# First attention divided by its row sums ahead of the transposes, and the first pair's operands loaded over two queues

## The chip, the cores and the metric

The kernel runs on one core of one Trainium2 chip. The metric is device time in microseconds of one execution, the median of several runs. The engines are named as the profile names them: PE is TensorE (its matmuls) and PEld its weight loads, DVE is VectorE, ACT is ScalarE, POOL is GpSimd, SP is SyncE; SPq and ACTq are the instruction queues of SP and ACT, from which DMAs are issued.

## What is computed

Two attentions in a row. The first has 8 batches of 8 heads, 576 rows of 64 elements, and keeps only scores within `tau` of the row's maximum; the second is a mixture of four single-head causal attentions, with a gate that picks two of them for each row.

```python
def _attn_ref(q, k, v, tau):                      # q, k, v: 8 x 8 x 576 x 64
    scores = scale * np.matmul(q, k.transpose(0, 1, 3, 2))
    thresh = np.max(scores, axis=-1, keepdims=True) - tau
    scores = np.where(scores >= thresh, scores, -1e9)
    attn = np.exp(scores - np.max(scores, axis=-1, keepdims=True))
    attn = attn / (np.sum(attn, axis=-1, keepdims=True) + 1e-09)
    return np.matmul(attn, v)
...
def _moe_ref(x, w_gate, wq, wk, wv, wo):          # x: 8 x 576 x 512, 4 experts
    ...
    for e in range(E):                            # causal attention per expert
        q, k, v = x @ wq[e], x @ wk[e], x @ wv[e]
        ...
        ye = a @ v @ wo[e]
        # added to out with the gate's weight where e is among the row's two best
```

## The kernel before

Work on the first attention goes by pair: two heads of one batch, 32 pairs in all (index `n`). A pair's queries and keys are loaded (`load`, line 304), transposed on PE (`tr_in`, line 1108) and split into a high and a low part (`prep`, line 314: `in_hi` and `in_lo` out of PSUM, or `in_raw`, `flat_hi` and `flat_lo` for pairs 1 to 5), because a product of two floats is made of three PE products, high by high, high by low and low by high. `scores(n, s)` (line 331) handles one of five tiles of query rows, in the order `TS = (4, 2, 3, 0, 1)`: tiles 0 to 3 are 128 rows for each of the two heads (two rows of work, `j` = 0 and 1, each 128 partitions by 576 keys), tile 4 holds the last 64 rows of both heads in one such row. That makes nine rows of 128x576 per pair, 288 in all. Each row is taken out of PSUM by DVE with its minimum (`s_min`, line 1175; keys are scaled negatively, so a minimum is the maximum), goes through exp on ACT (`s_exp`, line 1189), and is masked and summed on DVE by `s_stt` (line 1192, instruction at line 1194). The masked row is then transposed on PE (`tr_pp`, line 1239 by way of `turn`) and copied out of PSUM (`out_t`), and `attnv` (line 363) multiplies it with the values.

The division by the row sums is folded in afterwards. For each of the two groups of tiles of a pair, `GROUPS = ((4, 2, 3), (0, 1))`, the sums lie in a small buffer `sg`; `g_sum` adds the epsilon and `g_inv` inverts (line 1202), `g_wide` and `g_tail` spread the inverses over 128 columns each into `iw` (by way of `copy`), `tr_inv` transposes `iw` on PE (line 1077), `iv_out` copies it from PSUM into `iv`, and `x_mul` (line 1277) and `x_tail` (line 1281) multiply the transposed output of `av` by it while taking that out of PSUM. `x_hi`, `x_lo` and `x_two` split the product for the second attention.

`second(b)` runs after each batch's four pairs: projections, values, gate, scores, exp, a division of its own by row sums ahead of its transposes (`add_eps`, `inv`, `share`, `scale2` at line 1487), transposes, products with the values, and the output projection. Where both halves of the array write one accumulation (`crossed`, line 273), PE runs the first half, a tiny instruction on DVE, ACT or POOL (`fence`, line 1348) waits for it, and the second half waits for that.

The order of all instructions is written out by hand. Every task belongs to a family (`pt`, `iw`, `s`, ...); the table `ORDER` gives each task of a family its place in one global order, and `BY` gives one digit per task that names its engine where there is a choice. What a digit stands for follows from the call: for `evac` 0 is ACT and 1 DVE; for `moved` 0 POOL, 1 ACT, 2 DVE; for `small` and the fences 0 DVE, 1 ACT, 2 POOL; for the row scaling 0 POOL, 1 DVE, 2 ACT. `plan` (line 157) only assigns buffers and emits in that order, with some filler matmuls on PE during the first 23 us by its own count. Buffers are few: 8 PSUM banks (kinds `s` and `d` take two, `g` one) and the slots of `SLOTS`.

The first pair's keys are loaded by five DMAs from SP's queue, its queries by five from ACT's (line 306); all later loads go through SP. All of these DMAs are issued at line 1090.

## Time and profile before

| | |
|---|---|
| median of 3 runs | 832.75 us (831.75 to 833.85) |
| the profiled execution | 832.69 us |
| its span, first to last instruction | 831.0 us |
| granted TensorE clock, mean | 0.997 of full speed |
| busy share of the span | PE 97%, PEld 92%, DVE 88%, ACT 79%, POOL 34% |
| DMA | 43.18 MB, mean 52 GB/s |

A share of busy time is an average over the whole span; the stages of this kernel differ, and the rows below give them by stage. PE's matmuls are pipelined and their ends are modelled, so PE's busy time overstates what one group of matmuls costs the next; the starts of the weight loads (PEld) show at what pace PE moves on. Instructions of one engine may overlap by the fill of its pipeline, so a duration is a little longer than the step from one to the next.

### The profile page before, as it was taken

Reading aid. Unit: us, or ns where it says so; the run is one execution under the profiler, and the core shown is the slowest. Engines: PE = TensorE matmul, PEld = TensorE weight load, DVE = VectorE, ACT = ScalarE, POOL = GpSimd, SP = SyncE. Lnnn points to the kernel's source line nnn. Section 1 sums busy time; section 2 is a strip of 40 time slices with the busy share of each in tenths; the row PEclk is TensorE's granted clock in tenths of the full one; section 3 lists DMA queues with packets and bytes.
Section 4 is the critical chain, followed back from the end, with each engine's and each line's share of the span. In section 5 each row is a group of like instructions: output and inputs, shape, how many; then the busy total and the mean of one; then the engine's idle time right before and its main releaser. Section 6 shows DMA issues by size and latency. Waiting matters only on the chain.

```text
span 831.0 us, 35075 instructions
## 1 busy us (share of the span) xinstructions
PE 808.6 (97%) x14472; PEld 763.1 (92%) x14472; DVE 733.6 (88%) x2327; ACT 653.5 (79%) x1374; POOL 280.9 (34%) x604
## 2 busy tenths in 40 slices
PE   9989999999999999999999999999999999989998
PEld 7888999999989998899999999989998899988997
DVE  6999999998899889899988999998999988889474
ACT  4999779976898679887689767898679877779465
POOL 5756504412332124521235231521133422231451
PEclk9999999999999999999999999999999999999999
DMA  4433212122121212122112321113022113110002
GB/s 108 97 85 79 51 35 47 32 61 50 30 69 44 79 44 46 33 52 46 30 44 63 90 70 30 39 32 97 22 60 60 27 55 76 33 40 3 15 27 78
DMA packets 135632, 43.18 MB, mean 52 GB/s; under 512 B 130608, under 2 KB 130608, under 8 KB 135472
## 3 DMA queue, kind: packets, MB, share of 16 engines
q1 hardware_dynamic: 134240, 40.64, 20.1%
q8 instruction: 114, 1.87, 1.0%
q10 hardware_dynamic: 1232, 0.30, 0.2%
q14 instruction: 46, 0.38, 0.2%
HBM read 31.47 MB, written 9.44 MB: 49 GB/s over the span
## 4 chain that ended last, share of the span: by engine, by line
PE 75%; DVE 14%; ACT 7%; issue 3%; SPq 1%; DMA 1%; POOL 0%; DVEq 0%; ACTq 0%; POOLq 0%
PE ps L1087 61%; PE ps L1239 7%; PE ps L1077 6%; DVE e L1194 4%; DVE e L1177 4%; ACT pt L1063 2%; ACT e L1190 1%; DVE e L1464 1%; ACT e L1469 1%; SPq L1090 1%; DVE kk L1134 1%; DVE iv L1277 1%; ACT pa L1063 1%; DMA qi<-in_q_dram 0%; DVE pt L1065 0%
## 5 line engine op out<-in xcount | busy, mean ns | idle before, releaser
L1190 ACT ACTIVATE e<-e,sm 128x576 f32<-128x576 f32 x288 | 214.4, 770 | 24.0 <-DVE e L1177 23.2
L1177 DVE TENSOR_SCALAR_CACHE_REDUCE e<-ps 128x576 f32<-128x576 f32 x288 | 209.5, 752 | 21.4 <-PE ps L1087 16.6
L1194 DVE SCALAR_TENSOR_TENSOR e<-e,sm,e 128x576 f32<-128x576 f32 x256 | 204.7, 818 | 4.3 <-ACT e L1190 2.6
L1087 PE MATMUL ps<-kk,qq 64*128 64x288 f32 x1920 | 175.4, 306 | 3.1 <-DVE e L1177 1.8
L1063 ACT ACTIVATE pt<-ps 128x640 f32<-128x640 f32 (+3 forms) x234 | 146.5, 644 | 27.1 <-PE ps L1239 19.0
L1087 PE MATMUL ps<-pt,vm 128*64 128x128 f32 (+1 forms) x1536 | 155.9, 258 | 0.0
L1087 PEld LDWEIGHTS ps<-kk,qq 64*128 64x128 f32 x1920 | 141.2, 186 | 9.0 <-DVE e L1177 3.5
L1087 PE MATMUL ps<-pa,vm 128*64 128x128 f32 x1024 | 135.8, 276 | 1.0 <-DVE kk L1134 0.5
L1087 PEld LDWEIGHTS ps<-pt,vm 128*64 128x64 f32 x1536 | 131.1, 137 | 0.0
L1239 PE MATMUL ps<-ident,e 64*128 64x64 f32 x2624 | 124.2, 226 | 4.9 <-DVE e L1177 2.3
L1239 PEld LDWEIGHTS ps<-ident,e 64*128 64x128 f32 x2624 | 107.8, 139 | 14.9 <-DVE e L1177 4.3
L1087 PEld LDWEIGHTS ps<-pa,vm 128*64 128x64 f32 x1024 | 111.9, 137 | 6.1 <-DVE kk L1134 0.7
L1087 PE MATMUL ps<-x,wh 64*128 64x288 f32 x1024 | 106.6, 296 | 0.3 <-ACT pa L1063 0.2
L1087 PEld LDWEIGHTS ps<-x,wh 64*128 64x128 f32 x1024 | 86.1, 185 | 1.1 <-DVE e L1177 0.4
L1063 ACT ACTIVATE pa<-ps 128x512 f32<-128x512 f32 x114 | 67.0, 594 | 21.7 <-PE ps L1239 18.8
L1087 PE MATMUL ps<-x,wl 64*128 64x288 f32 x512 | 80.2, 292 | 0.0
L1492 POOL TENSOR_SCALAR e<-e,sm 128x384 f32<-128x384 f32 (+4 forms) x104 | 62.0, 604 | 36.8 <-DVE sm L1235 23.6
L1469 ACT ACTIVATE e<-e,sm 128x128 f32<-128x128 f32 (+3 forms) x128 | 70.8, 556 | 3.2 <-DVE sm L1464 2.8
L1464 DVE CUSTOM_DVE_ANT_0 e<-ps,tri 128x128 f32<-128x128 f32 (+3 forms) x128 | 58.7, 484 | 5.2 <-PE ps L1087 4.6
L1087 PE MATMUL ps<-wh,x 64*128 64x260 f32 x576 | 60.8, 285 | 0.0
L1071 POOL TENSOR_TENSOR x<-iv,x 128x64 fp32r<-128x64 f32 (+2 forms) x67 | 44.8, 678 | 41.9 <-ACT x L1063 27.9
L1087 PE MATMUL ps<-pt,vt 128*64 128x128 f32 (+1 forms) x640 | 58.9, 262 | 0.0
(163 smaller groups left out, 1650.2 us busy)
## 6 DMA issues: line engine op xcount, KB each, us to landing
vm<-in_v_dram SPq DMA_DIRECT2D x64, 128.0 KB, 2.6
out_dram<-ob SPq DMA_DIRECT2D x32, 256.0 KB, 2.4
ki<-in_k_dram SPq DMA_DIRECT2D x96, 64.0 KB, 2.4
qi<-in_q_dram SPq DMA_DIRECT2D x62, 80.0 KB, 2.4
ki<-in_k_dram SPq DMA_DIRECT2D x32, 80.0 KB, 2.5
vt<-in_v_dram SPq DMA_DIRECT2D x128, 16.0 KB, 2.1
qi<-in_q_dram SPq DMA_DIRECT2D x31, 64.0 KB, 2.3
qi<-in_q_dram SPq DMA_DIRECT2D x31, 48.0 KB, 2.5
```

Source lines behind the costliest of these rows:

```text
L1063: self.nc.scalar.activation(dst, src, AF.Copy)
L1071: eng.tensor_tensor(dst, a, b.bitcast(F32), op=ALU.subtract)
L1077: self.nc.tensor.transpose(self.ps[:, bank, c * n:(c + 1) * n], x[sl], self.ident[sl, sl])
L1087: return self.nc.tensor.matmul(out, x, y, start=first, stop=last)
L1090: (self.nc.sync if e == "SP" else self.nc.scalar).dma_start(dst, src)
L1177: self.nc.vector.tensor_scalar(self.sides(sc), self.dbank(s)[:, :, :HS], 0.0, None, op0=ALU.add, op1=ALU.min, accum_out=self.small(sm)[:, ...
L1190: self.nc.scalar.activation(self.row(e), self.row(sc), AF.Exp, bias=self.small(sm)[:, 2 * j:2 * j + 1], scale=-1.0)
L1194: self.nc.vector.scalar_tensor_tensor(self.row(e), self.row(sc), self.small(sm)[:, 8 + j:9 + j], self.row(e), op0=ALU.is_le, op1=ALU.mult, ...
L1239: self.nc.tensor.transpose(self.ps[:, g.slot + h, c * D:(c + 1) * D], x, self.ident[sl, sl])
L1464: self.nc.vector.tensor_tensor_reduce(self.row(p2)[:, :w], self.dbank(g)[:, j, :w], self.tri[:, SM - w:], 1.0, FAR, op0=ALU.add, op1=ALU.m ...
L1469: self.nc.scalar.activation(p, p, AF.Exp, bias=m[:, 2 * j:2 * j + 1], scale=-1.0, accum_out=m[:, 4 + 2 * j:5 + 2 * j])
L1492: (self.nc.vector if e == "DVE" else self.nc.gpsimd).tensor_scalar(p, p, x, 0.0, op0=ALU.mult, op1=ALU.add)
```

## The change

Three things are changed. First, each masked row of the first attention is divided by its own sum before it is transposed: `s_stt` puts its sum into the tile's small buffer `sm`, a step `eps1` adds the epsilon, `rec1` inverts on DVE, and `pn` multiplies the whole row of 576 in place on POOL, DVE or ACT, with the `scale2` that the second attention has. The spreading, transposing and copying of inverses goes away, with `sg` and `iw`, and `x_mul` becomes a plain copy out of PSUM, `xr`. Second, the first pair's loads may each go by SP or ACT, and `tau`'s too, and its transposes, high and low parts are done in two halves. Third, the whole of `ORDER` and `BY` is written anew. The long tables of `ORDER` and most of `BY` are left out below.

```diff
-    "ki": 1, "qi": 1, "vm": 2, "kk": 2, "qq": 2, "e": 8, "sg": 3, "iw": 1, "iv": 5, "rw": 2, "pa": 4, "pt": 8,
+    "ki": 1, "qi": 1, "vm": 2, "kk": 2, "qq": 2, "e": 8, "iv": 5, "rw": 2, "pa": 4, "pt": 8,
...
+    def scaling(w, fn, r, sm, buf, name):
+        x = task(None, {"POOL": (270 + 0.84 * w, 30), "DVE": (215 + 0.515 * w, 80), "ACT": (285 + 0.84 * w, 101)}, fn, [r], [], [sm, buf], name=name)
+        x.port = True
+        return x
...
-        e = "SP" if n else "ACT"
-        dk = [dma(lambda x=x: K.load_in(K.kis, K.k, n, *x, ki), (), [ki], move=72.0 * x[2], name=f"ldk.{n}") for x in KEYS]
-        dq = [dma(lambda x=x: K.load_in(K.qis, K.q, n, *x, qi, e), (), [qi], move=72.0 * x[2], name=f"ldq.{n}", e=e) for x in QUERIES]
+        e = "SP" if n else ("SP", "ACT")
+        into = lambda *a: (lambda: K.load_in(*a)) if n else lambda e: K.load_in(*a, e)
+        dk = [dma(into(K.kis, K.k, n, *x, ki), (), [ki], move=72.0 * x[2], name=f"ldk.{n}", e=e) for x in KEYS]
+        dq = [dma(into(K.qis, K.q, n, *x, qi), (), [qi], move=72.0 * x[2], name=f"ldq.{n}", e=e) for x in QUERIES]
...
+            if not n:
+                o = []
+                for y in range(2):
+                    m = pe(..., lambda ...: K.tr_in(g, tiles, src, (y,)), [z for z, a in zip(d, KEYS if scale else QUERIES) if a[-1] == y], [g, buf], [src], ..., name=f"t{f}.{n}")
+                    h = evac(WH + 80 * scale, lambda e, ...: K.in_hi(e, buf, g, scale, (y,)), [m, *(TAU[1:2] if scale else ())], [], [g, buf], name=f"{f}h.{n}")
+                    l = task("DVE", ..., lambda ...: K.in_lo(buf, g, scale, (y,)), [h], [], [g, buf], name=f"{f}l.{n}")
+                    o.append([h, l])
+                PREP[n] += [buf, o]
+                continue
...
-        th = small(lambda e: K.s_thr(e, sm, range(nj)), ms + ([] if n else TAU[2:]), sm, f"thr.{n}.{s}")
+        th = small(lambda e: K.plus(e, sm, 8, 0, nj), ms + ([] if n else TAU[2:]), sm, f"thr.{n}.{s}")
...
+        a = small(lambda e: K.plus(e, sm, 10, 4, nj), xs, sm, f"eps1.{n}.{s}")
+        r = task("DVE", SMALL, lambda: K.inv(sm, nj), [a], [], [sm], name=f"rec1.{n}.{s}")
+        ns = [scaling(S, lambda e, j=j: K.scale2(e, sm, ees[j], S, j), r, sm, ee, f"pn.{n}.{s}") for j in range(nj)]
+        for j in range(nj):
...
-            t = pe(..., lambda ...: K.tr_pp(g, ees[j], nc, s < R), xs if j == nj - 1 else [x], [g, pt], [ee], ..., name=f"tm.{n}.{s}")
+            t = pe(..., lambda ...: K.tr_pp(g, ees[j], nc, s < R), ns if j == nj - 1 else ns[:1], [g, pt], [ee], ..., name=f"tm.{n}.{s}")
...
-        a = task("DVE", SMALL, lambda: K.g_sum(sg, nt + nm), done, [], [sg], name=f"sum.{n}.{first}")
-        r = task("DVE", SMALL, lambda: K.g_inv(sg, nt + nm), [a], [], [sg], name=f"inv.{n}.{first}")
-        u = [moved(nm * P, lambda e: K.g_wide(e, sg, iw, nm), [r], [iw], [sg, iw], name=f"iw.{n}.{first}")]
-        if tail:
-            u.append(moved(P, lambda e: K.g_tail(e, sg, iw, nm), [r], [iw], [sg, iw], name=f"iw.{n}.{first}"))
-        t = pe(nt * TR + TX, lambda: K.tr_inv(gi, iw, nt), u, [gi, iv], [iw], "R", ld=76.0, kind="T", name=f"ti.{n}.{first}")
-        i = evac(nt * P, lambda e: K.iv_out(e, iv, gi, nt), [t], [], [gi, iv], name=f"iv.{n}.{first}")
+        iv = Buf("iv")
...
-        l = task("DVE", t_dve(w), lambda: K.x_mul(g, iv, w), [av, i], [], [g, iv], name=f"xm.{n}.{first}")
-        if tail:
-            l = task("DVE", t_dve(ST + 100), lambda: K.x_tail(g, iv, w), [l], [], [g, iv], name=f"xm.{n}.{first}")
+        l = evac(w, lambda e: K.x_raw(e, g, iv, w), [av], [iv], [g, iv], name=f"xr.{n}.{first}")
...
-    TAU.append(dma(K.load_tau, (), move=8.0, name="tau"))
+    TAU.append(dma(K.load_tau, (), move=8.0, name="tau", e=("SP", "ACT")))
...
-    "fs": "21120102222010020222200111112111",
-    "pt": "000000000000000000000000000000000000100000000000110000000000100000000000001000000001001001000000010000001000110000000000010000000100000000000100000111000100000000110000000000000001001001000000010000011000000000001000010000000100010000100000000100000000010000000000010100000000000000010100",
-    "iw": "010111111001012111000100021121110110111001120000211000001210001000001110010001000101010100011210",
-    "iv": "0000000000000010000001010000000000000101000000100000000110001101",
...
+    "tau": "100",
+    "fs": "12221201222222222200222002212212",
+    "eps1": "1222222222210210220112211200110212222011200120200121221120201010000000220201200201222101222212222022200100012122000000000200000200200021220000121210110222221200",
+    "pn": "202200220202020020211220002000220022020200002021020200200200000000020021122210022202000000020000000002020202220000202200222000001022000000200002212122102002200000000000000222001020000000022002210022012000020202020002002220022022202100002000122000020212221000120202020200200000000002000012",
+    "pt": "010000001000000000000001000000001000001000000001101000000000000000000001011000000010001010000010010000001000101100010000000100001000000000000001000011000000101100000100000001000000000000000001000000000000000010000101000001010001000000100000001010100101000000001000000000000000000000100001",
+    "xr": "0000000010010000010000000000000010100000000100001000000011100011",
...
+    def plus(self, e, sm, to, of, n):
+        m = self.small(sm)
+        ...
     def s_stt(...):
+        m = self.small(sm)
+        self.nc.vector.scalar_tensor_tensor(self.row(e), self.row(sc), m[:, 8 + j:9 + j], self.row(e), op0=ALU.is_le,
+                                            op1=ALU.mult, accum_out=m[:, 4 + 2 * j:5 + 2 * j])
...
+    def x_raw(self, e, g, iv, w):
+        self.copy(e, self.iv(iv)[:, :w], self.bank(g)[:, :w])
```

By the new tables SP issues, of the first pair's ten loads, keys 1, 4, 5 and 3 and query 3; ACT issues queries 1, 4, 5 and 2, key 2 and then `tau`. The 288 `pn` stand 170 on POOL, 99 on ACT and 19 on DVE; in the first four pairs it is 17, 17 and 2. The 160 `eps1` stand 65 on POOL, 34 on ACT and 61 on DVE (13, 4 and 3 in the first four pairs). Of 64 `xr`, ACT has 52; of 64 `iv` it had 53. The `pt` copies on DVE go from 38 to 47 (from none to 4 in the first four pairs). POOL's fences go from 49 to 57, `fs` among them from 12 to 22. The second attention's scalings on POOL go from 104 to 115.

## Rows read from the trace of the kernel before

**Rows 1.** The page's first part: busy us (share) x instructions, by engine.
```profile
PE 808.6 (97%) x14472; PEld 763.1 (92%) x14472; DVE 733.6 (88%) x2327; ACT 653.5 (79%) x1374; POOL 280.9 (34%) x604
```

**Rows 2.** Busy time by stretch: us, busy (x instructions), PE clock, DMA share, GB/s.
```profile
20.00:80.00 60.00, 55.61 (x1017) 50.51 (x1015) 57.32 (x172) 56.17 (x105) 36.80 (x60) 1.00 0.40 89
80.00:740.00 660.00, 650.24 (x11816) 617.75 (x11814) 606.18 (x1902) 528.91 (x1105) 203.72 (x446) 1.00 0.21 50
...
750.00:770.00 20.00, 19.41 (x372) 17.91 (x371) 19.26 (x69) 19.14 (x45) 4.31 (x8) 1.00 0.01 3
```

**Rows 3.** The same table for instructions that touch `iw` alone.
```profile
80.00:740.00 660.00, 18.75 (x264) 14.67 (x264) 1.54 (x6) 11.91 (x32) 15.06 (x41) 1.00 0.21 50
740.00:831.00 91.00, 1.36 (x20) 1.04 (x20) 0.29 (x1) 1.02 (x3) 0.82 (x2) 0.97 0.09 32
```

**Rows 4.** Timeline of weight loads: start us, us, engine, line, operation, out<-in, count.
```profile
407.92 0.26 PEld L1077 LDWEIGHTS ps<-ident,iw 64*128 64x128 f32 x6
408.10 0.44 PEld L1087 LDWEIGHTS ps<-kk,qq 64*128 64x128 f32 x6
```

**Rows 5.** Groups by form, removed steps: busy us, mean ns | idle before, releasers.
```profile
L1277 DVE TENSOR_TENSOR iv<-ps,iv 128x320 f32<-128x320 f32 x32 | 15.6, 487 | 3.6 <-PE ps L1087 2.4 <-ACT iv L1063 0.4 <-ACT e L1469 0.3
L1277 DVE TENSOR_TENSOR iv<-ps,iv 128x256 f32<-128x256 f32 x32 | 13.5, 420 | 4.5 <-PE ps L1087 2.6 <-issue 0.8 <-ACT iv L1063 0.6
L1281 DVE TENSOR_TENSOR iv<-ps,iv 64x64 f32<-64x64 f32 x32 | 7.3, 228 | 1.0
L1202 DVE RECIPROCAL sg<-sg 128x5 f32<-128x5 f32 x32 | 5.9, 184 | 0.3
L1063 ACT ACTIVATE iv<-ps 128x256 f32<-128x256 f32 x25 | 9.5, 378 | 5.2 <-PE ps L1077 4.5 <-PE ps L1239 0.6
L1063 ACT ACTIVATE iw<-sg 128x256 f32<-128x256 f32 x27 | 11.0, 408 | 0.9 <-ACT e L1190 0.5 <-DVE sg L1202 0.3
```

**Rows 6.** Groups by form, steps like those added or moved to another engine.
```profile
L1490 ACT ACTIVATE e<-e,sm 128x576 f32<-128x576 f32 x2 | 1.6, 776 | 1.2 <-POOL sm L1235 0.6 <-DVE sm L1235 0.5
L1492 POOL TENSOR_SCALAR e<-e,sm 128x576 f32<-128x576 f32 x13 | 10.4, 797 | 8.3 <-DVE sg L1058 7.1 <-DVE sm L1235 0.5 <-PE ps L1239 0.3
L1492 DVE TENSOR_SCALAR e<-e,sm 128x576 f32<-128x576 f32 x1 | 0.5, 512 | 0.0
L1230 DVE RECIPROCAL sm<-sm 128x2 f32<-128x2 f32 x64 | 9.9, 160 | 1.0
L1185 ACT ACTIVATE sm<-sm 128x2 f32<-128x2 f32 x26 | 7.5, 290 | 2.7 <-DVE e L1177 2.4
L1187 POOL TENSOR_TENSOR sm<-sm 128x2 f32<-128x2 f32 x51 | 16.9, 332 | 54.9 <-DVE e L1177 41.4 <-DVE sg L1058 8.0 <-DVE sm L1058 2.5
L1065 DVE COPY pt<-ps 128x640 f32<-128x640 f32 x26 | 21.2, 814 | 1.7 <-ACT q2d L1063 1.0 <-PE ps L1239 0.5
```

**Rows 7.** Masking steps on DVE: count, ns min/median/max; and one met by POOL, timeline.
```profile
L1194 DVE SCALAR_TENSOR_TENSOR e<-e,sm,e x256: 770/812/1399, 18.7 to 768.5; 128x576 f32<-128x576 f32 x128
...
142.85 0.82 DVE L1194 SCALAR_TENSOR_TENSOR e<-e,sm,e 128x576 f32<-128x576 f32 x1
...
142.93 1.36 POOL L1492 TENSOR_SCALAR e<-e,sm 128x576 f32<-128x576 f32 x1
```

**Rows 8.** Timeline of the start, columns as in rows 4.
```profile
4.51 0.50 SPq L1090 DMA_DIRECT2D ki<-in_k_dram  x1
7.17 0.39 PEld L1077 LDWEIGHTS ps<-ident,qi 64*128 64x128 f32 x10 [0.41 <-issue]
8.38 0.79 ACT L1124 ACTIVATE kk<-ps,qsc 128x640 fp32r<-128x640 f32 x1
9.25 0.88 DVE L1134 SCALAR_TENSOR_TENSOR kk<-ps,qsc,kk 128x640 fp32r<-128x640 f32 x1
10.19 1.28 PEld L1087 LDWEIGHTS ps<-kk,qq 64*128 64x128 f32 x17
```

**Rows 9.** Who waited for whom: us in total, times, longest.
```profile
PEld ps L1087 <- POOL fencePOOL L1353: 1.2, 4, 0.4
```

More of the change, by code (lines that the diff above doesn't have):

```diff
@@ L268, in dma @@
     def dma(fn, deps, takes=(), uses=(), move=576.0, name="", e="SP"):
-        x = task(e, (2000.0 + move, 1335.0 + move), fn, deps, takes, uses, name=name)
+        t = (2000.0 + move, 1335.0 + move)
+        x = task(e, t if isinstance(e, str) else {y: t for y in e}, fn, deps, takes, uses, name=name)
         x.move = move
@@ L318, in prep @@
             buf, g = Buf(cls), Buf("d")
+            if not n:
+                o = []
+                for y in range(2):
+                    m = pe((R + 1) * TR + TX, lambda g=g, src=src, tiles=tiles, y=y: K.tr_in(g, tiles, src, (y,)), [z for z, a in zip(d, KEYS if scale else QUERIES) if a[-1] == y], [g, buf], [src], "R", ld=76.0, kind="T", name=f"t{f}.{n}")
+                    h = evac(WH + 80 * scale, lambda e, g=g, buf=buf, scale=scale, y=y: K.in_hi(e, buf, g, scale, (y,)), [m, *(TAU[1:2] if scale else ())], [], [g, buf], name=f"{f}h.{n}")
+                    l = task("DVE", t_dve(WH + 60 * scale), lambda g=g, buf=buf, scale=scale, y=y: K.in_lo(buf, g, scale, (y,)), [h], [], [g, buf], name=f"{f}l.{n}")
+                    o.append([h, l])
+                PREP[n] += [buf, o]
+                continue
             raw = Buf("pt") if 0 < n < NLO else None
             m = pe((R + 1) * TR + TX, lambda g=g, src=src, tiles=tiles: K.tr_in(g, tiles, src), d, [g, buf, *([raw] if raw else [])], [src], "R", ld=76.0, kind="T", name=f"t{f}.{n}")
-            m = [m, *TAU[1:2]] if scale and not n else [m]
+            m = [m]
             if raw:
@@ L332, in scores @@
         kk, dk, qq, dq = PREP[n]
+        if not n:
+            dk, dq = sum(dk, []), [x for y in ((0,), (0,), (0, 1), (1,), (1,))[s] for x in dq[y]]
         nj = 2 if s < R else 1
         sm = Buf("sm")
-        if (n, group(s)) not in SUMS:
-            SUMS[n, group(s)] = (Buf("sg"), [])
-        sg, done = SUMS[n, group(s)]
         bufs = [Buf("s") for _ in range(nj)]
@@ L340, in scores @@
         scs, ees = [(sc, j) for j in range(nj)], [(ee, j + 2 - nj) for j in range(nj)]
-        takes = [*bufs, *dict.fromkeys((sc, ee)), sm, sg]
+        takes = [*bufs, *dict.fromkeys((sc, ee)), sm]
         if s < R:
@@ L480, in score @@
             r = task(None, {"DVE": SMALL, "POOL": (197, 30)}, lambda e: K.share(e, sm, gw, t, ep, nj), [r, *gd], [], [sm, gw], name=f"shr.{name}")
-            ns = [task(None, {"POOL": (270 + 0.84 * w, 30), "DVE": (215 + 0.515 * w, 80), "ACT": (285 + 0.84 * w, 101)}, lambda e, j=j: K.scale2(e, sm, p2[j], w, j), [r], [], [sm, pb], name=f"p2s.{name}")
-                  for j in range(nj)]
-            for x in ns:
-                x.port = True
+            ns = [scaling(w, lambda e, j=j: K.scale2(e, sm, p2[j], w, j), r, sm, pb, f"p2s.{name}") for j in range(nj)]
             return p2, ns
@@ L1106, in load_vt, with tr_in @@
         self.dma(self.vts[vm.slot][HEADS[j ^ x], x, j], self.v[b, 2 * hp + j, SM:, :])
-    def tr_in(self, g, tiles, buf):
+    def tr_in(self, g, tiles, buf, hs=(0, 1)):
         for c in range(R + 1):
-            self.transpose(g, c, tiles[buf.slot][:, c].rearrange("p j d -> p (j d)"))
+            x = tiles[buf.slot][:, c].rearrange("p j d -> p (j d)")
+            for h in hs:
+                self.turn(g, c, x[HEADS[h]], h)
     def kq(self, buf):
@@ L1215, in tr_inv, with s_stt @@
-    def tr_inv(self, g, iw, n):
-        for c in range(n):
-            self.transpose(g, c, self.iw(iw)[:, c])
+    def s_stt(self, sc, sm, e, j):
+        m = self.small(sm)
+        self.nc.vector.scalar_tensor_tensor(self.row(e), self.row(sc), m[:, 8 + j:9 + j], self.row(e), op0=ALU.is_le,
+                                            op1=ALU.mult, accum_out=m[:, 4 + 2 * j:5 + 2 * j])
     def iv(self, buf):
-        return self.t(buf, [P, 3 * P])
-    def iv_out(self, e, iv, g, n):
-        self.copy(e, self.whole(self.iv(iv)[:, :n * P]), self.halves(g, n))
+        return self.t(buf, [P, 2 * P + ST])
```

264 lines of the change are left out of this document (113 added, 151 removed), and 293 rows, old and new, of the table ORDER.

## The prediction

> **What bounds the kernel now.** I read the page's busy shares first [rows 1]: PE 97%, DVE 88%, ACT 79%, POOL 34%. An average hides the stages, so next the table of busy time by stretch [rows 2]. From 80 to 740 us first and second attention run side by side, and PE is busy 650.2 of 660 us, 98.5%, with DVE at 91.8%, ACT at 80.1% and POOL at 30.9%. Only 9.8 us of PE's time there is idle, so that stretch is about as long as PE's own work. From 20 to 80 us only the first four pairs run; there DVE is at 95.5% and ACT at 93.6%, while PE is at 92.7% with filler matmuls counted in. That stretch belongs to DVE and ACT, not to PE. From 750 to 770 us, the end of the last pairs, DVE and ACT are at 96.3% and 95.7%, and PE at 97.1%. So a saving on PE is worth its full size in the long stretch alone, and work added to ACT or DVE costs something at both ends.
>
> The base of the sum is the profiled execution, 832.7 us, of which 831.0 us are span and 1.7 lie around it. The median, 832.75, is the same within 0.1.
>
> **PE: ten transposes per pair go.** The transposes of `iw` are 320 instructions, 264 of them between 80 and 740 us and 20 after that [rows 3]. Their weight loads are busy 14.67 + 1.04 = 15.7 us there, and that is the upper bound. The lower one is the pace: six start at 407.92, and the next group's loads start at 408.10 [rows 4], so six take 0.18 us, 0.03 each; 284 x 0.03 = 8.5 us. In this group the loads themselves are busy 0.26 us, of which 0.08 lie beside the next group's. The truth is between, because some groups stand where PE has to wait or to change over. I take -11, nearer to the pace. Nothing else on PE changes in number: the masked rows are transposed as before, the first pair's transposes are the same ones in two halves. The work after 770 us is the second attention's own and stays.
>
> **The long way round the other engines.** Removed from DVE, per pair: the multiplications 0.487 + 0.420 + 0.228 [rows 5], and two sums and two inversions, four at most 0.184 each [rows 5], together some 1.8 us. Added: five inversions of 0.160, five `eps1`, of which 61 in 160 stand on DVE, some 0.160 each as the inversion, 19/32 of a 0.512 us scaling, and 9/32 of a `pt` copy of 0.814 [rows 6]: 0.80 + 0.31 + 0.30 + 0.23 = 1.6 us, and 12/64 of two `xr` copies, about as long as the multiplications, 0.2. DVE comes out even. POOL gains 170 scalings, at 0.797 in the mean, and 65 `eps1` of 0.332 [rows 6], and loses 47 spreadings, a good 0.4 each by ACT's 0.408 [rows 5]: 135.5 + 21.6 - 19 = +138 us, on a POOL that is 34% busy [rows 1]. ACT gains 99 x 0.776 + 34 x 0.290 = 86.7 us [rows 6] and loses 42 spreadings of 0.408 [rows 5] at most and nine `pt` copies, about as long as DVE's 0.814 [rows 6]: 17 + 7; its `xr` copies replace its `iv` copies, 52 for 53, of like width. So +62 us on 653.5, 79% to 86%. All of it is hidden behind PE as long as PE is the late one.
>
> Each row's chain gets longer too, by an `eps1`, an inversion and a scaling, 0.3 + 0.2 + 0.8 us [rows 6]. PE takes its instructions in a fixed order, so a late scaling holds up the transposes and everything queued behind them. On ACT a scaling stands in front of exps and PSUM copies, on POOL in front of fences, which the second half of a crossed product waits for; those waits cost 1.2 us in all now [rows 9], and 57 fences instead of 49 then sit behind steps of 0.8 us. What all these waits cost on PE after 80 us no row shows. If PE's fill falls from 98.5% to the 97.1% that it has between 750 and 770 us, beside DVE and ACT as full as there [rows 2], it is 660 x 0.014 = +9. Below nothing it could be -3, a third of the 9.8 us idle now, since the inverses no longer hold two PSUM banks and the product of `av` leaves its bank without waiting for `iv`. DVE stays at 91.8% and ACT gets to about 529 + 0.825 x 62 = 580 of 650 us, 89%, which is between the rows for 80 to 740 and 750 to 770 us and nearer to the first: I take +2.
>
> **The first four pairs.** By the new table 17 of their 36 scalings stand on ACT, 17 on POOL and 2 on DVE, so ACT gets 17 x 0.776 + 4 x 0.290 = 14.4 us and loses eight spreadings of at most 0.408 and four `pt` copies: some +8 net. DVE gets 20 x 0.160 + 2 x 0.512 + 4 x 0.814 + 3 x 0.160 = 8.0 and loses 4 x 1.8 = 7.2: even or a little more. ACT has 56.2 of 60 us busy there [rows 2]. To hold 64.2 at the 95.7% that it reaches between 750 and 770 us the stretch would have to be 67.1 us long: +7. At the other end it is 0, if the added work is put off into the next stretch, where ACT has room. I take +3: the second attention can't start before the fourth pair is through, but not all ACT work of this stretch belongs to those pairs.
>
> **The start.** Now the last key load is issued at 4.51, PE starts on the queries at 7.17, and ACT does the keys' high part only at 8.38, DVE the low one at 9.25; the score products run from 10.19 [rows 8]. SP now issues six loads with `tau` among them; after the change SP issues five and ACT five and then `tau`, so SP's later loads (values, weights) move up by one issue and ACT's table load moves down by one, ahead of its first copy at any rate. Halves let DVE take the low part of one half while ACT does the high part of the other: of 0.79 + 0.88 us [rows 8] about half lies side by side, 0.8 us, and I give the earlier loads 0.2. I take -1.0, from 0 (the `tau` behind five loads on ACT is the late one then) to -1.5.
>
> **The sum.** 832.7 - 1.0 (start) + 3.0 (first pairs) - 11.0 (PE) + 2.0 (waits) = 825.7 us, 0.8% faster.
>
> **The rivals.** *POOL and DVE get in each other's way: slower.* A masking step on DVE reads two rows from SBUF. At 142.85 one ran beside a POOL scaling that took 1.36 us [rows 7]; the mean of its kind is 0.797 [rows 6]. The longest masking step took 1.40 us where the median is 0.81 [rows 7]. So a meeting costs one of the two some 0.5 us. The Trainium skill (SBUF — State Buffer, section "SBUF: two separate sides") says that the two engines hold a shared pair of ports exclusively for a whole instruction, and whoever starts later is fully blocked; the meeting at 142.85 agrees. After the change 170 + 115 scalings stand on POOL. From 80 to 740 us DVE has 606 us busy; at the 96.3% fill of the stretch from 750 to 770 us, a stretch of 651 us holds 627, so 21 us, 42 meetings of 0.5 on DVE's side, are free, and from there on each costs time. At 80 meetings DVE needs 646/0.963 = 671 us, 20 more than 651: 825.7 + 20 = 846. For it speaks POOL's doubled load; against it that the masking steps' median and minimum are 0.81 and 0.77 [rows 7], so meetings are rare beside the 104 scalings and other steps of today.
>
> *The gain is given back as waits: no change.* If both unknown terms go near their upper ends, +6 for the first pairs and +8 for waits, it is 832.7 - 1 - 11 + 6 + 8 = 834.7. For it speaks that where ACT and DVE are both full PE is not [rows 2], and that weight loads fill only 617.8 of 660 us of the long stretch, 93.6%, so PE has more slack than its matmuls show. The Trainium skill (Perfetto Trace Analysis, section "Identifying the Most-Contended Engine") holds matmul busy time a poor measure of headroom and asks for the weight loads' share; by it the long stretch is less firmly PE's, and more of the 11 us would be lost. Against it speaks that ACT would still be at 89%.
>
> *PE gets more than I take: faster still.* With the upper bound of 15.7 and no added waits: 832.7 - 1 + 3 - 15.7 - 3 = 816.
>
> *The loading does not do what it says.* If the first score products start no earlier, the forecast moves by +1.0, to 826.7; it lies inside the forecast.
>
> **How the numbers follow.** The forecast, 818 to 830, gets 0.55; the still faster case 0.08; waits taking the gain (829 to 838) 0.22; POOL against DVE 0.15. About 0.3% of the time, 2.5 us, is what a measurement can tell from no change: faster is below 830.2, slower above 835.2. Faster: 0.55 + 0.08 and 0.02 of the 0.22, 0.65. Same: 0.12 of the 0.22. Slower: 0.15 and the other 0.08, 0.23. The range goes from 814, which holds the still faster case, to 838, the upper end of the case of waits; left out are most of POOL against DVE and a little below 814, under 0.2. The likeliest case's own range is 818 to 830.
>
> **What the profile would show.** No `iw` on any engine, and PE with 320 transposes fewer; between 80 us and the end of the first attention PE's busy share still at 98% or above, in a stretch some 8 to 11 us shorter. The first score products at about 9.2 instead of 10.19. The second attention's first projection up to 3 us later. Masking steps with a mean below 0.85; a mean near 1.0 would show the meetings. PE's waits on POOL's fences and on scalings below 4 us in all. I am wrong if PE's share in the long stretch falls to 97% or below, or if the second attention's start slips by more than 6 us.

## The result, and the profile after

| | before | after |
|---|---|---|
| median, runs side by side | 833.3 us (831.75 to 834.32, 4 runs) | 821.66 us (821.08 to 821.99, 4 runs) |
| ratio, 95% interval | | 0.9861 (0.9843 to 0.9879) |
| span of the profiled execution | 831.0 us | 820.2 us |
| granted TensorE clock, mean | 0.997 | 0.993 |

The changed kernel is 1.4% faster. That is inside the range and on the side that was forecast; the gain in span is 10.8 us, where the sum had 7.0. The page's first row, and the group that it lists first, after the change, answer to [rows 1] (busy us, share, instructions; the group: busy us, mean ns, idle before it):

```profile
PE 798.4 (97%) x14145; PEld 752.8 (92%) x14145; DVE 724.4 (88%) x2326; ACT 697.3 (85%) x1437; POOL 433.0 (53%) x833
...
L1474 POOL TENSOR_SCALAR e<-e,sm 128x576 f32<-128x576 f32 (+4 forms) x285 | 195.6, 695 | 95.6 <-DVE sm L1216 58.0
```

PE has 327 matmuls fewer in the records; the change takes away 320, and a trace can lack a few records. POOL gained 152 us (138 forecast), ACT 44 (62), and DVE lost 9 (even). By stretch, as in [rows 2] (us, busy (x instructions) of PE, PEld, DVE, ACT, POOL, then PE clock, DMA share, GB/s), the changed kernel:

```profile
10.00:20.00 10.00, 9.95 (x90) 8.98 (x91) 7.50 (x20) 5.65 (x11) 4.44 (x6) 0.66 0.27 61
...
20.00:80.00 60.00, 54.60 (x936) 49.07 (x933) 58.01 (x170) 57.37 (x100) 56.69 (x85) 0.97 0.37 82
80.00:730.00 650.00, 641.13 (x11590) 608.96 (x11586) 593.50 (x1896) 569.72 (x1170) 328.78 (x635) 1.00 0.21 50
...
740.00:760.00 20.00, 19.52 (x372) 18.16 (x372) 18.84 (x67) 19.20 (x44) 12.03 (x21) 1.00 0.01 2
```

In the long stretch PE is busy 641.1 of 650 us, 98.6%: it is still the late one, beside an ACT at 87.7% (89 was forecast) and a POOL at 50.6%. From 20 to 80 us POOL goes from 36.8 to 56.7 of 60 us, and in the 10 us before, PE's clock is granted at 0.66 in the mean.

Two marks split the span: the first minimum that DVE takes, and the first weight load of the second attention's first projection and of its last. They are read from the timelines; "middle" lies between the first and the last of these projections.

| kernel | first minimum | first projection | middle | rest | span |
|---|---|---|---|---|---|
| before | 11.35 | 85.8 | 693.6 | 51.6 | 831.0 |
| after | 12.45 | 91.2 | 677.4 | 51.7 | 820.2 |
| difference | +1.1 | +5.4 | -16.2 | 0 | -10.8 |

So the change loses 5.4 us before the first projection and wins 16.2 behind it. The same table of busy time, cut at these marks, for the kernel before:

```profile
11.35:85.80 74.45, 69.30 (x1226) 62.82 (x1224) 70.71 (x207) 65.74 (x122) 47.81 (x80) 1.00 0.38 84
...
85.80:779.40 693.60, 681.81 (x12376) 646.58 (x12372) 633.68 (x2008) 558.65 (x1179) 212.03 (x462) 1.00 0.20 47
```

and for the changed one:

```profile
12.45:91.20 78.75, 72.68 (x1197) 65.53 (x1195) 74.25 (x213) 72.14 (x126) 68.45 (x107) 0.95 0.34 74
...
91.20:768.60 677.40, 668.30 (x12094) 633.90 (x12092) 618.53 (x1997) 595.58 (x1235) 345.29 (x664) 1.00 0.20 48
```

In the middle the weight loads (second busy number) are busy 646.6 before and 633.9 after, 12.7 less; what is left of the length, in which PE loads nothing, is 47.0 before and 43.5 after, 3.5 less. The two make up the 16.2. In the first stretch the engine to look at is DVE (third number): 70.7 of 74.45 us before, 74.25 of 78.75 after, 95% and 94%. Its work grew by 3.5 us and its idle time by 0.8, which is the 4.3 us by which that stretch is longer. Such a sum can be made for any engine, so by itself it does not show that DVE sets the length; f and c below bear on that.

### The profile page after: what moved, and what is told of

It reads as the page before. It is cut to its first block, busy times and chain, and to the rows that moved or that the text cites. A ratio compares the mean times of both kernels' runs of the same rounds, so it can differ in the third digit from the quotient of the medians.

```text
span 820.2 us, 34773 instructions
## 1 busy us (share of the span) xinstructions
PE 798.4 (97%) x14145; PEld 752.8 (92%) x14145; DVE 724.4 (88%) x2326; ACT 697.3 (85%) x1437; POOL 433.0 (53%) x833
## 4 chain that ended last, share of the span: by engine, by line
PE 69%; DVE 7%; ACT 6%; issue 2%; POOL 1%; DVEq 0%; ACTq 0%
PE ps L1094 57%; PE ps L1225 9%; PE ps L1084 3%; DVE e L1188 2%; ACT pt L1070 2%; DVE e L1205 1%; ACT e L1201 1%; ACT e L1451 1%; DVE pt L1072 1%; ACT pa L1070 1%; DVE e L1446 1%; POOL e L1474 0%; DVE kk L1145 0%; ACT kk L1133 0%; ACT e L1472 0%
## 5 line engine op out<-in xcount | busy, mean ns | idle before, releaser
L1474 POOL TENSOR_SCALAR e<-e,sm 128x576 f32<-128x576 f32 (+4 forms) x285 | 195.6, 695 | 95.6 <-DVE sm L1216 58.0
L1094 PE MATMUL ps<-kk,qq 64*128 64x288 f32 x1920 | 180.2, 308 | 4.7 <-POOL fencePOOL L1335 1.6
L1094 PEld LDWEIGHTS ps<-kk,qq 64*128 64x128 f32 x1920 | 145.3, 188 | 13.7 <-POOL fencePOOL L1335 2.1
L1070 ACT ACTIVATE pt<-ps 128x640 f32<-128x640 f32 (+3 forms) x232 | 144.3, 641 | 14.2 <-PE ps L1225 9.2
L1198 POOL TENSOR_TENSOR sm<-sm 128x2 f32<-128x2 f32 (+1 forms) x128 | 44.0, 346 | 99.4 <-DVE e L1205 58.2
L1472 ACT ACTIVATE e<-e,sm 128x576 f32<-128x576 f32 (+4 forms) x121 | 88.0, 736 | 8.8 <-DVE sm L1216 8.3
L1451 ACT ACTIVATE e<-e,sm 128x256 f32<-128x256 f32 (+3 forms) x128 | 71.0, 558 | 1.9 <-DVE sm L1446 1.7
L1070 ACT ACTIVATE pa<-ps 128x512 f32<-128x512 f32 x105 | 61.9, 594 | 5.2 <-PE ps L1225 4.1
L1335 POOL TENSOR_SCALAR fencePOOL<-eps 128x2 f32<-128x2 f32 x57 | 17.6, 309 | 87.8 <-PE ps L1094 86.2
L1446 DVE CUSTOM_DVE_ANT_0 e<-ps,tri 128x384 f32<-128x384 f32 (+3 forms) x128 | 58.3, 484 | 3.8 <-PE ps L1094 2.1
```

What stands on the lines that cost most here:

```text
L1070: self.nc.scalar.activation(dst, src, AF.Copy)
L1094: return self.nc.tensor.matmul(out, x, y, start=first, stop=last)
L1198: self.nc.gpsimd.tensor_tensor(m[:, to:to + n], m[:, of:of + 2 * n:2], m[:, of + 1:of + 2 * n:2], op=ALU.add)
L1446: self.nc.vector.tensor_tensor_reduce(self.row(p2)[:, :w], self.dbank(g)[:, j, :w], self.tri[:, SM - w:], 1.0, FAR, op0=ALU.add, op1=ALU.m ...
L1451: self.nc.scalar.activation(p, p, AF.Exp, bias=m[:, 2 * j:2 * j + 1], scale=-1.0, accum_out=m[:, 4 + 2 * j:5 + 2 * j])
L1472: self.nc.scalar.activation(p, p, AF.Copy, scale=x)
```

## The experiments

Each was timed beside the kernel before on the same chip (832.67, 832.22 or 832.35 us by the group of runs). Each has a letter, which stands with its edit. The theory to be tested: PE's own work is what the middle loses, and the added work on POOL and ACT is hidden. Its rivals: the gain comes from the new order as such, or from the chain on the other engines.

**The transposes of the inverses alone.** In the kernel before, PE leaves them out (e; `iv` is then copied from PSUM that holds something else, so the rows are not divided by their sums), or does them twice (d).

```diff
 def tr_inv(...):                      # e
-        for c in range(n):
-            self.transpose(g, c, self.iw(iw)[:, c])
+        pass
 def tr_inv(...):                      # d
-        for c in range(n):
+        for c in [*range(n), *range(n)]:
```

> The kernel before without the 320 transposes of the inverses; spreading, copying out of PSUM (of what happens to lie there) and multiplying stay, so the first attention is not divided by its sums. All engines but PE do what they did before. The changed kernel gained 16.2 us between its first and its last projections. Theory (these transposes cost PE their whole step from one weight load to the next group's, changes of kind and waits with them, 18.3 us in 320): 833 less 14 to 18, 815 to 819, and the middle stretch shorter by 13 to 17. Rival (they cost their pace alone, 0.03 us each, and the rest of the gain comes from elsewhere, from shorter chains, PSUM banks or the new order): 833 less 8 to 11, 822 to 825.

> The kernel before with each transposition of the inverses done twice in a row, 320 instructions more on PE, 284 of them after 80 us, with no new change of kind and no new wait. Theory (the pace is 0.03 us an instruction, and PE is the bound after 80 us): 8.5 to 10 us more than before, 841.5 to 843.5; what the changed kernel gained beyond that, 16.2 - 8.5, is then changes of kind and waits. Rival (PE has slack that its matmuls hide): under 5 us more.

Without them: 828.05 us, ratio 0.9941 (0.9927 to 0.9956); twice: 839.02 us, 1.0086 (1.0067 to 1.0106). The middle of each, without and twice:

```profile
86.60:774.80 688.20, 674.24 (x12096) 635.97 (x12092) 632.35 (x2008) 556.67 (x1178) 214.29 (x462) 1.00 0.20 48
```

```profile
86.20:785.90 699.70, 688.92 (x12658) 654.35 (x12654) 634.44 (x2008) 558.90 (x1179) 210.59 (x462) 1.00 0.19 47
```

Taking 280 transposes out of the middle takes 10.6 us off the weight loads, 0.038 each; adding about as many adds 7.8, 0.028 each. The forecast's pace of 0.03 and its choice of -11 stand, as time of weight loads. But of the 10.6 only 5.4 reach the length of the middle: the time without a weight load rises from 47.0 to 52.2. With the order held, half of the gain turns into waits. Of the 7.8 that are added, 6.1 reach it. The median fell by 4.6 us without the transposes, two fifths of what the whole change wins, and rose by 6.8 with them twice. Both lie outside what was expected: e falls short of its theory and of its rival, and d lies between the two.

**The whole division, in the old order and in the new.** In the kernel before, all steps of the division are left out (i: sums, inversions, spreading, transposes, copies; `x_mul` is a copy). In the changed one (j), the order stays and `eps1`, `rec1` and `pn` issue nothing. Neither divides.

```diff
 # i: g_sum, g_inv, g_wide, g_tail, tr_inv, iv_out, x_tail -> pass
-        self.nc.vector.tensor_tensor(self.iv(iv)[:, :w], self.bank(g)[:, :w], self.iv(iv)[:, :w], op=ALU.mult)
+        self.copy("DVE", self.iv(iv)[:, :w], self.bank(g)[:, :w])
 # j
-        ... lambda e: K.plus(e, sm, 10, 4, nj) ... lambda: K.inv(sm, nj) ... lambda e, j=j: K.scale2(e, sm, ees[j], S, j)
+        ... lambda e: None ... lambda: None ... lambda e, j=j: None
```

> The kernel before without any division of the first attention: sums, inversions, spreadings, transposes and copies of the inverses are left out, the product of av is only copied out of PSUM by DVE. Between first and last projection the kernel before takes 693.6 us, 646.6 of them with weight loads busy and 47.0 without; without the transposes alone it was 688.2, 636.0 and 52.2; the changed kernel has 677.4, 633.9 and 43.5. Theory (the waits fell because the order was written anew for less PE work; the other engines' removed steps were hidden): weight loads idle for 48 us or more, 684 to 688 in that stretch, 824 to 828 in all. Rival (the chain of inversions on the other engines held PE up, and its removal is the gain): idle 44 or less, 677 to 680, 817 to 820 in all.

> The changed kernel without its added steps (no epsilon, no inversion and no scaling of the first attention's rows), so undivided too, in the order of the changed kernel. Theory (the added 200 us on POOL and ACT are hidden in the order that was written around them): first to last projection 674 to 677, 1 to 3 us below the changed kernel there, and 2 us less up to the first projection, 816 to 819 in all. Rival (the added steps hold PE up much as they did when they were doubled, by 0.6 to 0.8 us for each one): 660 or less in that stretch, 800 to 806 in all.

The first took 820.83 us, 0.9861 (0.9846 to 0.9876); the second 820.4, 0.9852 (0.9831 to 0.9873). Their middles:

```profile
84.00:766.60 682.60, 670.82 (x12098) 634.56 (x12094) 610.33 (x1850) 533.95 (x1099) 199.70 (x419) 1.00 0.20 48
```

```profile
91.00:767.60 676.60, 667.01 (x12092) 633.75 (x12090) 596.47 (x1783) 539.83 (x1124) 229.07 (x461) 1.00 0.20 48
```

Put in a row by the time without a weight load, these give the middle's whole account. Old order, transposes gone, chain kept: 52.2. Old order, chain gone too: 48.0. New order, nothing of either division: 42.9. New order with all added steps: 43.5. So the changed kernel's middle, with 116 us more on POOL and 56 more on ACT than the undivided one beside it, is 0.8 us longer than it and 5.2 shorter than the old order with no division at all. In the middle the added work is hidden to within a microsecond, as the theory says; and the waits that the missing transposes would have left (5.2) were taken back by the missing chain (4.2) and by the rest of what was ordered anew (5.1). What in the new tables gave the 5.1 was not taken apart: the tables of all families changed at once. Of i's two expectations neither came out (its middle of 682.6 lies between them); j's middle is as its theory has it, its whole time 1.4 us above. And over the whole kernel the new order as such wins nothing: the two undivided kernels take 820.83 and 820.4 us, because the first projection comes at 91.0 in the new order and at 84.0 in the old. What the new order gains behind that mark, it loses ahead of it.

**More work in the new order.** Scalings from the fifth pair on are done twice where they stand on POOL (g), or where they stand on ACT (h); those rows are divided twice.

```diff
-        ns = [scaling(S, lambda e, j=j: K.scale2(e, sm, ees[j], S, j), ...
+        ns = [scaling(S, lambda e, j=j: [K.scale2(...) for _ in range(2 if n >= NPAIR and e == "POOL" else 1)], ...
```

> The changed kernel with the scalings of the first attention that stand on POOL done twice from the fifth pair on (rows divided twice): 153 steps of 0.75 us more on POOL, about 115 us. Theory (POOL at about half load has room and meetings with DVE stay rare because the order keeps them apart): POOL at 67%, 1 to 5 us more than the changed kernel, 823 to 827. Rival (each meeting costs DVE 0.5 us, and twice the steps can't be kept apart): masking steps at a mean over 0.90 us, 832 or more.

> The changed kernel with the scalings of the first attention that stand on ACT done twice from the fifth pair on (rows divided twice): 82 steps of 0.77 us more, 63 us, on an ACT that is busy 570 of 650 us between 80 and 730 us. Theory (ACT is then at 97% and takes the bound from PE, or makes PE wait): 8 to 20 us more than the changed kernel, 830 to 842. Rival (ACT's steps stay hidden behind PE as in the change itself): under 4 us more.

POOL twice: 907.63 us, 1.0925 (1.0889 to 1.0962). ACT twice: 863.88 us, 1.0384 (1.0356 to 1.0413). The middle with POOL twice:

```profile
91.30:857.40 766.10, 696.77 (x12092) 653.55 (x12090) 641.12 (x1998) 602.45 (x1235) 473.06 (x817) 0.97 0.18 43
```

PE's waits in the same execution (who waited, for whom: us, times, longest):

```profile
PEld ps L1225 <- POOL e L1474: 60.4, 63, 4.0
PEld ps L1094 <- POOL fencePOOL L1335: 12.5, 10, 2.6
```

The middle with ACT twice, and PE's waits:

```profile
91.00:810.00 719.00, 682.36 (x12092) 637.73 (x12090) 620.73 (x1997) 651.52 (x1316) 344.45 (x664) 1.00 0.19 45
```

```profile
PEld ps L1225 <- ACT e L1472: 10.6, 20, 1.5
PEld ps L1094 <- ACT pt L1070: 8.7, 26, 1.1
```

POOL's work in the middle rises by 127.8 us and the middle by 88.7, 69% of it, though POOL is then only 62% busy. ACT's rises by 55.9 and the middle by 41.6, 74% of it. Both are far above what was expected (1 to 5 and 8 to 20 us); g's rival allowed for it (832 or more), but not by the way it named, as the masking steps below show. The first scaling of each row, 116 us on POOL and 56 on ACT, cost 0.8 us in the middle (j); a second one on POOL alone costs two thirds of its length. That the order was written with the first ones in it is my explanation, and it is not shown: a chain that has room for one scaling and not for two would look the same, and no run puts single scalings into an order that was written without them. PE's idle time in the middle of g is 112.5 us instead of 43.5, and its weight loads, the same in number, take 19.6 us longer, beside a granted clock of 0.97: part of them ran at half speed.

**Do POOL and DVE get in each other's way?** This is the forecast's rival that ends slower, and g is its strongest case. Masking steps by form, as [rows 6] has its groups, before, in the changed kernel and with POOL twice (busy us, mean ns, idle before):

```profile
L1194 DVE SCALAR_TENSOR_TENSOR e<-e,sm,e 128x576 f32<-128x576 f32 x256 | 204.7, 818 | 4.3 <-ACT e L1190 2.6
```

```profile
L1205 DVE SCALAR_TENSOR_TENSOR e<-e,sm,e 128x576 f32<-128x576 f32 x256 | 205.2, 828 | 6.0 <-ACT e L1201 3.2 <-POOL kk L1078 0.4 <-ACT sm L1196 0.2
```

```profile
L1205 DVE SCALAR_TENSOR_TENSOR e<-e,sm,e 128x576 f32<-128x576 f32 x256 | 220.0, 885 | 10.0 <-POOL sm L1198 5.5 <-ACT e L1201 2.7
```

The mean was 818 ns before and is 828 now: 2.6 us over 256 steps. Counted in the timelines, 8 of 288 masking steps lasted over 0.95 us before, 9 after, 45 with POOL twice. The rival needed 42 meetings; the changed kernel has about as many as the old one. In g the steps grew by 14.8 us, a sixth of what its middle lost. How busy POOL is does not decide the number: j, with the least work on POOL in the new order (229 us in the middle), has 25 such steps and a mean of 848 ns. It goes by when the steps fall.

**The first four pairs' scalings.** In the changed kernel those of the first batch are left out (f); its rows are not divided.

```diff
-        ns = [scaling(S, lambda e, j=j: K.scale2(e, sm, ees[j], S, j), ...
+        ns = [scaling(S, lambda e, j=j: n < NPAIR or K.scale2(e, sm, ees[j], S, j), ...
```

> The changed kernel without the 36 scalings of the first four pairs (these are left undivided). The first projection came at 91.2 instead of 85.8 us. Theory (ACT, DVE and POOL are all full there, and the scalings are what made the stretch longer): first projection 3 to 5 us earlier, the whole 817 to 819. Rival (the late start and the half clock did it): first projection under 1 us earlier, the whole 821 to 822.

It took 819.98 us, 0.9853 (0.9833 to 0.9873). Its first projection comes at 89.3 us, 1.9 earlier than with the scalings, and the middle is 677.2. Its first stretch:

```profile
12.33:89.30 76.97, 71.33 (x1195) 64.48 (x1193) 72.33 (x210) 61.82 (x109) 50.87 (x90) 0.97 0.35 77
```

Without the 17 scalings on ACT and 19 elsewhere, ACT has 10.3 us less to do and the stretch is 1.8 shorter; DVE has 1.9 less. So the length does not go with ACT. The result lies between the theory and the rival. With all added steps gone (j) the stretch is still 77.5 us long, 3.1 longer than before. So by these two executions less than half of the 4.3 us are the added steps. The rest lies in the new order of these pairs or in the new start: c, below, has the old order with the new start, and its stretch is 77.4 us long with DVE's work as before (70.9 us) and at full clock.

**The start.** Four kernels: the table load of ACT early in the changed kernel (a, one tiny activation moved up); the same with `tau` loaded first, by SP (k); the changed kernel with the old loading and preparing of the first pair (b); the kernel before with the new one (c).

```diff
 ORDER["warm"]                          # a and k
-        717,
+        15.5,
 ORDER["tau"], BY["tau"]                # k: first entry 15 -> 0.5, "100" -> "000"
 ORDER and BY of tk, kh, kl, tq, qh, ql, ldk, ldq, tau: the first pair's entries of the other kernel,
 with the branch `if not n` (halves) taken out (b) or put in (c)
```

> The changed kernel with one thing moved: the warming exp of ACT, and so the load of its function table, stands right behind ACT's six DMA issues instead of at place 717. In the changed kernel the table load sits behind the wait for tau (7.69 to 8.97 us) and the first score products start at 9.98, with most of them from 10.61; TensorE is then granted half its clock from 10.0 to 16.9 and from 30.5 to 33.9 us. Theory (the start was lost to the table load): the key's high part at about 7.7 instead of 8.98, first score products about 9.2, the first row's minimum at about 11.0 instead of 12.45, and 1.0 to 3 us off the whole, 818.5 to 820.7. Rival (the first four pairs are held by DVE, ACT and POOL anyway, so a late start is made up): within 0.5 us of 821.7.

> The changed kernel with ACT's table load behind its DMA issues, as in the run with that alone, and with tau issued by SP second of all, right after the first key load, instead of by ACT last of all. With the table load alone the first minimum came at 10.97 and the first projection at 88.7, and the keys' high part waited for tau until 8.25. Theory (these waits, and not the work, are what the new start lost): the keys' high part at 7.3 to 7.8, first minimum at about 10.3, no half clock before 20 us, first projection at 88 or earlier, the whole 2 to 4 us below the changed kernel. Rival (only the single profiled executions differed): within 1 us of the changed kernel.

> The changed kernel with the start of the kernel before: keys and tau by SP, queries by ACT, transposes and parts of the first pair in one piece. Theory (the second part of the change costs rather than gains, 1.1 us at the first minimum and more by the half clock): first minimum at 11.3 instead of 12.45, no half clock before 40 us, 1 to 3 us off, 818.5 to 820.7. Rival (the loss up to the first projection, 85.8 to 91.2 us, is all from the scalings): 821.7 within 0.5.

> The kernel before with the start of the changed one alone (ten loads and tau over two queues, first pair in halves). Theory: first minimum 1.1 us later, at about 12.4, and the whole 1 to 3 us longer than before, 834 to 836 beside 833. Rival (as I predicted: halves and two queues start the score products earlier): 832.

| kernel | us | ratio (interval) | first minimum | first projection | middle |
|---|---|---|---|---|---|
| a, table early | 820.7 | 0.986 (0.9847 to 0.9873) | 10.97 | 88.7 | 677.3 |
| k, table and `tau` early | 822.64 | 0.9887 (0.9872 to 0.9901) | 10.07 | 91.4 | 677.5 |
| b, old start, new order | 822.94 | 0.9891 (0.9877 to 0.9906) | 11.01 | 91.5 | 677.5 |
| c, new start, old order | 836.51 | 1.0061 (1.0037 to 1.0085) | 11.82 | 89.2 | 694.1 |

The timeline of the changed kernel's start, to be read against [rows 8] (start us, us, engine, line, operation; in brackets the idle time before it and what ended it):

```profile
4.21 0.62 ACTq L1097 DMA_DIRECT2D tau_t<-in_tau_dram  x1
...
7.45 0.15 DVE L1029 TENSOR_SCALAR qsc<-tau_t 128x1 f32<-128x1 f32 x1 [0.23 <-DMA tau_t<-in_tau_dram]
...
7.69 1.28 ACT L1133 ACT_TABLE_LOAD   x1 [7.69 <-DVE qsc L1029]
...
8.98 0.94 ACT L1133 ACTIVATE kk<-ps,qsc 128x320 fp32r<-128x320 f32 x2
...
9.98 0.26 PEld L1094 LDWEIGHTS ps<-kk,qq 64*128 64x128 f32 x1 [0.98 <-ACT kk L1133]
...
12.45 0.76 DVE L1188 TENSOR_SCALAR_CACHE_REDUCE e<-ps 128x576 f32<-128x576 f32 x1 [0.90 <-PE ps L1094]
```

and ACT's two first steps before, and with the tiny activation ahead:

```profile
4.22 1.28 ACT L1063 ACT_TABLE_LOAD   x1 [4.22 <-issue]
7.78 0.70 ACT L1063 ACTIVATE qq<-ps 128x640 fp32r<-128x640 f32 x1 [2.27 <-PE ps L1077]
```

```profile
4.86 1.28 ACT L1036 ACT_TABLE_LOAD   x1 [4.86 <-DMA qi<-in_q_dram]
...
8.25 0.94 ACT L1133 ACTIVATE kk<-ps,qsc 128x320 fp32r<-128x320 f32 x2 [1.89 <-DVE qsc L1029]
```

Before, ACT's first activation read transposed queries, and its table load ran at 4.22, long before they were there: it did not wait for what its activation waited for until 7.78. Now the first activation needs both the transposed keys from PE and the scale that DVE makes from `tau`. In the trace ACT's queue has a wait of its own for the scale, which ends at 7.6, and the table load stands behind that one: it runs at 7.69, and its 1.28 us are all on the path. With the load out of the way (a) the keys' high part comes 0.73 us earlier, bounded by `tau` (landed shortly before 7.99), and the first minimum comes 1.5 us earlier, at 10.97. That is 0.4 us ahead of the kernel before, but executions with the old start and the old order have it at 10.63 to 11.41 (before, d, e, i), so no gain of loading in halves is shown by it. Those of the changed kernel's start have it at 12.29 to 13.47 (after, f, g, h, j and the changed kernel again): later in every one. In c, with the late table load and no half clock, it is 11.82. With the table early and `tau` first (k) it is 10.07.

But an earlier start is kept only in a. In k the first projection comes no earlier than in the changed kernel, and in the median k is no faster. The steps of DVE show where its lead goes: the sixteenth minimum comes at 36.1 us in k, 36.7 in a and 39.6 in the changed kernel, the nineteenth at 45.5, 42.8 and 45.3. In between, PE stands still in k from 32 us on, and then runs slow; the timeline:

```profile
34.43 0.75 DVE L1188 TENSOR_SCALAR_CACHE_REDUCE e<-ps 128x576 f32<-128x576 f32 x1
...
35.24 0.18 PEld L1094 LDWEIGHTS ps<-pa,vm 128*64 128x64 f32 x1 [2.91 <-DVE e L1188]
```

and the row of busy time around it, columns as above:

```profile
30.00:40.00 10.00, 6.38 (x94) 6.18 (x96) 6.67 (x21) 6.18 (x12) 7.87 (x12) 0.83 0.39 88
```

2.9 us pass before the first product with the values. What ends them is DVE's minimum step, which ran until 35.18; the load of the values, issued at 27.96, had landed 2.5 us later. The minimum step takes a score tile out of PSUM, so this reads as a wait for its bank. From 35.0 to 38.4 us, beginning while PE still stands, the clock is at its lower level, 1.2 GHz instead of 2.4. b shows the same stop (2.92 us) and the same half clock, against its expectation. In a and in the changed kernel the same product waits for ACT instead, less than 0.1 us, and starts in a at 32.94; a's half clock falls from 26.7 to 30.1. So a keeps its lead of 2.5 us up to the first projection because it does not meet this stop. In the median that is 820.7 against 821.66, and the intervals of the ratios lie over each other; b's is clear of a's. By the medians, the new start without the new order costs 0.6% (c), and taking it out of the new order costs about 0.3% or nothing (b).

**The changed kernel again**, beside k, i and j:

> The changed kernel as it is, for a comparison on one chip with the next. 821 to 822, first projection at about 91, first to last projection 677.

822.05 us, 0.9869 (0.9853 to 0.9886), with the marks at 12.62 and 91.3 and a middle of 677.4. Single executions of the changed kernel, here and above, had spans of 817.7 to 820.4 us; the middle repeats to 0.1 us, so differences of 2 us in the first 90 are near what one execution can tell. None of the variants that divide as the reference does is measurably faster than the changed kernel.

## Why the prediction was right, and where its terms were not

| term of the sum | forecast (bounds) | measured |
|---|---|---|
| start, to the first minimum | -1.0 (-1.5 to 0) | +1.1 |
| first four pairs, to the first projection | +3.0 (0 to +7) | +4.3 |
| PE's own work | -11.0 (-15.7 to -8.5) | -12.7 |
| waits behind it | +2.0 (-3 to +9) | -3.5 |
| sum | -7.0 | -10.8 |

The two terms at the start came out 3.4 us worse than forecast, the two behind them 7.2 better. That the whole lies well inside the range is thus in part luck: the errors have opposite signs.

*PE.* The reading that the long stretch is PE's, and that a transpose is worth about its pace there, held: d prices one at 0.028 us and e at 0.038, and the fill stayed at 98.6%. Of the -12.7, e has 10.6; the other 2.1 came with the missing chain (i, 1.4) and the new order. The middle got shorter by 16.2, more than the 8 to 11 that the forecast wanted to see, because the waits fell too.

*Waits.* This step failed, just beyond its lower bound. I worked it out from the fill beside fuller engines, as if the old order were kept; and e shows that with the old order the waits do rise, by 5.2. That is the mechanism of the rival in which the gain is given back, and it took half of it. What the forecast put no higher than its lower bound is that the sums, the spreading and the copies were waits of PE's too (e against i, 4.2); what it left out is that a new order is more than the added steps in it (i against j, 5.1). The waits that I did watch for did come up. In the changed kernel, over the whole span:

```profile
PEld ps L1225 <- POOL e L1474: 6.2, 17, 1.1
...
PEld ps L1094 <- POOL fencePOOL L1335: 2.1, 2, 1.6
```

8.3 us together, where below 4 was forecast; the fences cost 2.1 instead of the 1.2 of [rows 9]. Others fell by more. The Trainium skill (Perfetto Trace Analysis, section "Identifying the Most-Contended Engine") asks for the weight loads' share in place of matmul busy time. Here the two differ: by matmul busy time (681.8 and 668.3 in the middle) PE's work fell by 13.5 and its idle time by 2.7, and e idles 2.2 us more than the kernel before; by the weight loads e idles 5.2 more. No run here shows which of the two is nearer.

*The first four pairs.* The size was inside its bounds, but the step that gave it failed: I let ACT set this stretch. ACT's work rose by 6.4 us, near the 8 of the forecast, but f shows that 10 us off ACT shorten the stretch by 1.8. DVE is the fullest engine there, and for DVE I had found "even or a little more": it rose by 3.5. By line, DVE took over five copies out of PSUM (3.8 us; I had counted four `pt` copies and no other), its 21 inversions cost 3.3, and its 34 main masking steps took 878 ns each instead of 840, 1.3 us, beside a POOL that is busy 68.45 of 78.75 us here; against that stand the multiplications (4.5), group sums (1.2) and group inversions (1.4) that went. The largest item I had not counted at all: by the new table DVE makes 14 low parts in this stretch (line 1078) instead of 7, 7.3 us instead of 3.3. But that DVE's work sets the length is not shown. In c the stretch is 2.9 us longer with DVE's work as before, and in seven of the nine executions in the new order the first projection comes at 91.0 to 91.5 us, with the first minimum anywhere from 10.07 (k) to 13.47 (j, which has none of the added steps). What holds it there stays open, but for the stop in k and b.

*The start.* Wrong in sign. The failed step is the clause that the table load "moves down by one, ahead of its first copy at any rate". It is still ahead of the first copy, but behind a wait. The rival that the loading does not do what it says came true in a worse form: one weight load for the score products runs at 9.98, about where it ran before, the other seventeen from 10.61 instead of 10.19, where 9.2 was forecast, and PE's clock is at half from 10.0 to 16.9 us, after a stop of 0.98; a second such stretch follows from 30.5 to 33.9.

*POOL against DVE.* The rival needed 42 meetings; outside the first pairs they did not get more. POOL's share of 50.6% in the long stretch did not bring it about; in g, where POOL is at 62%, 45 steps were long. The Trainium skill (SBUF — State Buffer, section "SBUF: two separate sides") says that the later of the two is blocked for the whole instruction. The longest masking step after agrees: it took 1.47 us where the median is 0.81, and began at 23.92, 0.01 us behind a POOL step of 0.87 (a low part, not a scaling). Such meetings were as few as before, so the rival's price for one was about right, and its number of them was not.

## What to carry to other kernels

In a kernel with a fixed order, split PE's time at marks that both kernels have, and each part into weight loads and the rest: work and waits then show apart, and an edit made with the order held, as in e, tells how much of a saving the order gives back. A half idle engine is not free: in the order of the changed kernel one scaling per row was hidden, and a second brought two thirds (POOL) to three quarters (ACT) of its length into the time. Before moving a load of a constant to ACT's queue or changing ACT's first activation, look in the trace at where the table load then runs: it can come to stand behind a wait of that activation.

## What the runs showed of the hardware

The table load of 1.28 us stands right ahead of the first activation in ACT's order and need not run at the first free moment: it ran at 4.22 us where that activation waited for PE alone, 3.56 us ahead of the activation itself; at 7.69 where the activation needed PE and DVE, behind the wait for DVE; and at 4.86 with a tiny activation put ahead.

Some short stops of PE in the first 40 us were followed by the lower clock, and others about as long were not. 0.98 us without a weight load before 9.98 was followed by half clock to 16.9, and 2.91 before 35.24 in k had it from 35.0 to 38.4; but behind 0.94 before 9.24 in a (full clock to 26.7) and 2.09 before 35.37 in c (full clock to 90 us at least) there was none. A start that was 2.4 us earlier (k) was lost by the stop and the half clock, and by the 3.9 us that DVE then waited for PE at 40.75; no run here shows what another order of the first loads would keep of it.
